# One two-bank PSUM tile for every second pair of units, or two tiles of one bank each

## The chip, the cores and the metric

The kernel runs on one core of a Trainium2 chip. Its time is device microseconds (us) from start to end of one execution; the time before is the median of three runs. The profile and its trace come from one more execution. Engines are written as the profile writes them: PE (TensorE, matmuls), PEld (its weight loads), DVE (VectorE), ACT (ScalarE), POOL (GpSimd) and SP (SyncE, which issues most DMAs). PSUM, the memory that matmuls write, has eight banks of 512 float32 columns on each of 128 partitions.

## The reference

Three layers follow each other; the output is that of the last.

```python
# 1. linear attention with a delta rule: B=4, H=8, S=768, D=48
k_n = k / (norm(k) + 1e-6); state = zeros(B, H, D, D)
for t in range(S):
    y[t] = q[t] @ state
    state += beta[t] * outer(k_n[t], v[t] - state.T @ k_n[t])
# 2. x: 3072 tokens x 384; hidden layer of 2048 with a rational activation
h = x @ w_in
g = (a0 + a1*h + a2*h*h + a3*h*h*h) / (1 + |b0|*|h| + |b1|*h*h + 1e-6)
x = g @ w_out
# 3. 8 experts (384 -> 1024 -> 384, ReLU); each token goes to one expert, at most
#    384 tokens an expert, given out greedily from the highest logit downwards
out[mask_e] = relu(x[mask_e] @ w1[e]) @ w2[e]
```

## The kernel before, in words

The sequence is cut into 12 chunks of 64 steps, so a chunk has 256 tokens (4 batches). The attention of a chunk is a dozen groups of small float32 matmuls into the PSUM tile `tg` (two banks), each read back by ACT or DVE before the next group can use it. It gives the chunk's `xT`. The hidden layer of a chunk is done in 8 **units** of 256 hidden features, 96 units in all. One unit is, in this order:

- `h`, line 906: 18 matmuls of 256 columns (fp16 high and low halves, three products) into the unit's own PSUM tile `P` of one bank;
- the activation, 128x512 at a time, on ACT and DVE by turns. From `P`: L892 `w` (ACT), L889 `q` (ACT), L895 `q` (DVE), L898 and L899 `w` (DVE). Then `P` is used as scratch: L877 and L878 write it (ACT), L881 reads it (DVE), L879 writes it (DVE) and L883 reads it for the last time (DVE). L896 works on `q` alone;
- `gg`, the fp16 high half on ACT (L869) and the low half on DVE or POOL (L870);
- `x2`, line 853: 12 matmuls that add to the chunk's output in `px` (two banks).

A unit takes about four steps of the software pipeline, so four `P` tiles are in use by turns. Units 0 and 1 of each four take the two buffers of a pool, named `ph` in the profile, one bank each. Units 2 and 3 take the halves of `rec`, **one tile of two banks**, cut in two by slicing (`rec0`, `rec1`):

```python
bk[n]=pool.tile([128,1024],F32,name=n)                                    # L1448, n = "tg", "rec"
for i in range(2): bk["%s%d"%(n,i)]=bk[n][:,512*i:512*i+512]
```

While chunk 0 is prepared, `rec` as a whole holds the results of attention groups; its last such use is chunk 0's output `y`, read by ACT and DVE (L1434, L1435) into `xs`. From the first unit with number 2 on, `rec` holds halves only.

The order of the instructions on each engine is set when the kernel is built, by a planner (`Sched`) with a table of durations and priorities; it treats the halves as two banks that have nothing to do with each other. The semaphores are added later by a framework that looks at which instructions write and read which tile. POOL solves small triangular systems for pairs of chunks (L203, L204), with the results going through DRAM (`dA` in, `dW` out). Fill-in matmuls without use (`hot`, L1454) keep PE busy in some of its waits in the first part.

The execution has these parts: up to 67.8 us no unit runs; from 73.8 us (first matmul of a unit into `rec`) to 246 us units of chunks 0 to 2 run beside the preparation of weights; from 246 to 636 us eight chunks, 3 to 10, run in a regular loop; the last chunk's units end by about 690 us; then routing and experts, which use no `rec`.

Of the kernel before, what the change touches and what calls it, by code (L numbers as in the profile page):

```python
# [7 lines left out]
F32 = mybir.dt.float32  # L8
# [6 lines left out]
PSUM = bass.MemoryType.PSUM  # L15
# [495 lines left out]
class Ring:  # L511
# [7 lines left out]
    px=[-381.55,-1154.14,-2703.93,-1331.31,375.89,-100.94,-55.85,-813.57],  # L519
# [206 lines left out]
class Experts:  # L726
# [27 lines left out]
    def split(s,n,q,x,xn,h,l,hn,ln,sc):  # L754

        g=s.g; nc=s.nc; p=PR['sp'][n]+PR['sq'][n]*q
        g.add(('ACT',.43,lambda: nc.scalar.activation(h,x,AF.Copy,scale=sc)),[xn],[hn],p)
        g.add(('DVE',.47,lambda: nc.vector.scalar_tensor_tensor(l,x,sc,h,op0=OP.mult,op1=OP.subtract)),[xn,hn],[ln],p+PR['sl'][n])  # L758
# [84 lines left out]
def units(g,M,T,u0,xT,newP,NP,O):  # L843
# [72 lines left out]
    half=7,  # L916
# [158 lines left out]
def prologue(g,A,M,xT,yev,pack,stg,stx,bk):  # L1075

    nc=A.nc; te,ac,ve,po,sp=nc.tensor,nc.scalar,nc.vector,nc.gpsimd,nc.sync; T={}; LPF=[False]
# [14 lines left out]
    def mm(dur,fn,banks,r,w,pr,act=None):  # L1092

        box=[]
        def f():
            o=A.tg,A.rec; A.tg,A.rec=Banks(),Banks(); A.tg.q,A.rec.q=[bk[b] for b in banks if b[0]=='t'],[bk[b.replace('rt','t')] for b in banks if b[0]=='r']; M.tg=A.tg; A.pend=[]; fn(); A.tg,A.rec=o; M.tg=A.tg; box.extend(A.pend); A.pend=[]
        add(('PE',dur,f),r,w,pr,act=act); return box
    def ev(box,k,eng,dur,r,w,pr): add([('DVE',.6,lambda: box[k](False)),('ACT',.5,lambda: box[k](True))] if eng=='AD' else (eng,dur,lambda: box[k]()),r,w,pr)
# [104 lines left out]
    b=mm(1.7,a12,['rec'],['tn','Ut1'],RE,c0,act=256); ev(b,0,'ACT',.6,RE,['X'],c0)  # L1203
    b=mm(1.7,lambda: A.comb2(0),['rec'],['X',('TT',1),('TT',3)],RE,c0,act=256)
    ev(b,0,'ACT',.55,RE,[('TT',4)],c0); ev(b,1,'AD',.6,RE,[('TT',5)],c0)
    b=mm(2.3,lambda: A.tr(0),['tg'],TD+[('V',0)],TG,cr,act=3072)
# [96 lines left out]
        ev(b,0,'DVE',.081,['tg0'],[('Lt',c)],PP['xo']+8)  # L1303
    id16=A.id16; o,o1=Opt(),Opt(); o.N=DM if ONE else DX; o.K=3; o.stop=False; o.new=o1.new=lambda n,un: M.wk.tile([128,512],F32,name=n,bufs=Opt.R[n]); o.XP,o.HP,o.QP,o.GP,o.SP,o.wi,o.wo=PP['XP'],PP['HP'],PP['QP'],PP['GP'],(0,9),lambda fb,j: [('wi',fb//4,j),('xT',0)],lambda fb: [('wo',fb)] if ONE else [('wo',fb),('wgl',fb)]
    o1.N=DX; o1.K=3; o1.stop=False; o1.XP,o1.HP,o1.QP,o1.GP,o1.SP,o1.wi,o1.wo=PP['XP1'],PP['HP1'],PP['QP1'],PP['GP1'],(0,9),lambda fb,j: [('xT',1)],lambda fb: [('wgl',fb)] if ONE else []
    def newP4(un): return M.ph.tile([128,2,256],F32,name="ph") if un%4<2 else bk['rec%d'%(un%2)].rearrange("p (a b) -> p a b",b=256)
    o.PQ=o1.PQ=PP['PQ']
    U_=[units(g,M,T,0,lambda: xT[0],newP4,4,o),units(g,M,T,8,lambda: xT[1],newP4,4,o1)]; hv=(0,1)
    first=len(g.t)
    add(('DVE',.7,lambda: A.comb0(1)),TD[:4],['tn'],s1_[0])  # L1310
# [11 lines left out]
    for c in range(2):  # L1322
        st=step(c+1)
        for u in range(8):
            un=8*c+u
# [89 lines left out]
def body(ctx,tc,q,k,v,beta,w_in,w_out,a,b,w_gate,w1,w2,out):  # L1415
    nc=tc.nc
    ctx.enter_context(tc.manual_schedule())
    per=ctx.enter_context(tc.tile_pool(name="per",bufs=1))
    drm=ctx.enter_context(tc.tile_pool(name="x2dram",bufs=1,space=DRAM))
    x2d=drm.tile([B*S,DM],F32,name="x2d")  # L1420
    Lt=per.tile([128,E,NT],F32,name="Lt"); nc.gpsimd.memset(Lt,0.0)
    keep=ctx.enter_context(tc.tile_pool(name="keep",bufs=1)); ppx=ctx.enter_context(tc.tile_pool(name="ppx",bufs=2,space=PSUM))
    with ExitStack() as ph1:
        tg=ph1.enter_context(tc.tile_pool(name="ptg",bufs=1,space=PSUM))
        rec=ph1.enter_context(tc.tile_pool(name="prec",bufs=1,space=PSUM))
        pph=ph1.enter_context(tc.tile_pool(name="pph",bufs=2,space=PSUM))
        n=NCK*128*1024; A=Att(ph1,tc,q,(k[0:n].rearrange("(a b) -> a b",b=1024),k[n:].rearrange("(a b) -> a b",b=U*48)),v,beta,tg,rec)
        M=Moe(ph1,tc,w_in,w_out,a,b,w_gate,tg,pph,ppx,keep)
        xw=ph1.enter_context(tc.tile_pool(name="xw",bufs=2))
        xT={}  # L1430
        def yev(c,P,k):
            if c and k==0: xT['s']=xw.tile([128,2,1024],F16,name="xs",bufs=1)
            hi,lo=[xT['s'][:,i] for i in range(2)]; src=P.rearrange("a r p t -> a (r p t)")
            if k==0: nc.scalar.activation(hi,src,AF.Copy,scale=XS)  # L1434
            else: nc.vector.scalar_tensor_tensor(lo,src,XS,hi,op0=OP.mult,op1=OP.subtract)  # L1435
        def pack(c):
            xs=xT['s'].rearrange("p l (s t) -> p l s t",s=4)
            x=xT[c]=xw.tile([128,2,3,256],F16,name="xT")
            for o,n,a,j,i in ((0,48,0,slice(0,3),slice(0,3)),(48,48,64,slice(0,3),slice(0,3)),(96,32,0,0,3),(96,16,32,1,3),(112,16,64,1,3),(96,32,80,2,3)): nc.sync.dma_start(x[o:o+n,:,j],xs[a:a+n,:,i])
        warm=xw.tile([128,256],F16,name="warm",bufs=1); nc.vector.memset(warm,0.0)  # L1440
        M.pools(ph1)
        with ExitStack() as pro:
            ws=pro.enter_context(tc.tile_pool(name="mws",bufs=1,side="right"))
            M.ws=ws; stx=ws.tile([128,FF//2,2],I32,name="wsi")
            stg=[M.wk.tile([128,512],F32,name=n,bufs=b) for n,b in (("sa",2),("sa",2),("q",2),("q",2),("w",3),("w",3),("w",3),("y",2),("y",2))]
            xT['s']=xw.tile([128,2,1024],F16,name="xs",bufs=1); bk={}
            for n,pool in (("tg",tg),("rec",rec)):
                bk[n]=pool.tile([128,1024],F32,name=n)  # L1448
                for i in range(2): bk["%s%d"%(n,i)]=bk[n][:,512*i:512*i+512]
            A.bk=bk  # L1450
            for n,pool,tag in (("P",pph,"ph"),("px",ppx,"px")):
                for i in range(2): bk["%s%d"%(n,i)]=pool.tile([128,512],F32,name=tag)
            def hot(n,t=None):
                for _ in range(n): nc.tensor.matmul((bk['px1'] if t is None else t)[:,0:256],warm[:,0:128],warm,start=True,stop=True)  # L1454
            hot(H00)
            g=Sched(); g.nc=nc; g.tol=PP['tol']; g.free.update(SP=0.6,POOL=3.2,DVE=2.5,ACT=2.0,PE=2.5)
            g.x2d,g.Lt=x2d,Lt; g.mid=lambda: hot(2); T,i1=prologue(g,A,M,xT,yev,pack,stg,stx,bk); i0=next(i for i,t in enumerate(g.t) if t[0][0][0]=='PE'); i1=max(i for i in range(len(g.t)) if g.t[i][0][0][0]=='PE')
            run(g,hot,i0,i1,0,HM,HG,[(('px',1),bk['px1'])]+[(b,bk[b]) for b in ('tg0','tg1')]+[(('P',2+i,0),bk['rec%d'%i]) for i in range(2)])
        rc=ctx.enter_context(tc.tile_pool(name="rc0",bufs=1,side="right"))
        def route():  # L1460
            T['R']=Route(ctx,tc,rc); T['R'].Lt=Lt
        e=g.end; on=g.on; z={x: max([e[i] for i in range(len(e)) if on[i]==x]) for x in ('PE','DVE','ACT','POOL')}; g2=Sched(); g2.nc=nc; g2.x2d,g2.Lt=x2d,Lt; g2.tol=LP['tol']; g2.free.update({x: max(0.0,z[x]-z['PE']+1.0) for x in z})
        T['loop'](g2,route)
        def emit(t,i,f):
            if f: f()
        g2.run(emit); R=T['R']; un=8*(NCK-1)
        G1={un-1: (T['q',un-1],T['w',un-1],T['P',un-1].rearrange("p a b -> p (a b)"))}; G2={un-2: T['w',un-2]}; G3={un-3: T['gg',un-3]}; PX={NCK-2: T['px',NCK-2]}
        g=R.g=Sched(); g.nc=nc
        i0,i1,T=drain(g,M,A,R,(G1,G2,G3,PX[NCK-2]),xT[NCK-1],x2d,Lt); spare=[]
        def hot(n):  # L1470
            if n and not spare: spare.append(M.ph.tile([128,2,256],F32,name="ph"))
            for _ in range(n): nc.tensor.matmul(spare[0][:,0],R.one,warm2,start=True,stop=True)
        warm2=R.hotx
        run(g,hot,i0,i1,EH)
    with ExitStack() as ph2:
        rps=ph2.enter_context(tc.tile_pool(name="rps",bufs=1,space=PSUM))
        eph=ph2.enter_context(tc.tile_pool(name="eph",bufs=1,space=PSUM))
        R.rings(ph2,rps)
        X=Experts(ph2,tc,w1,w2,out,x2d,eph,T['px',NCK-1],M.wof_)
        R.late(ph2)  # L1480
        nc.gpsimd.tensor_scalar(X.ident,R.jp,0.0,None,op0=OP.is_equal); nc.gpsimd.tensor_scalar(X.neg,X.ident,-1.0,None,op0=OP.mult)
        g=tail(R,X,M,T); g.nc=nc; g.free['POOL']=6.0; g.free['ACT']=2.0
        def hot(n):
            for _ in range(n): nc.tensor.matmul(X.ph.t[3][:,:256],R.one,warm2,start=True,stop=True)
        run(g,hot,0,X.first)


body = with_exitstack(body)

_INS = ["q", "k", "v", "beta", "moe_w_in", "moe_w_out", "moe_a", "moe_b", "moe2_w_gate", "moe2_w1", "moe2_w2"]  # L1490
# [58 lines left out]
```

## Time and profile before

| | |
|---|---|
| runs | 970.15 us median (969.09, 970.15, 974.95) |
| profiled execution, its own time | 968.28 us |
| its span, first to last instruction | 966.5 us |
| granted TensorE clock, mean | 0.959 of full |
| PE / DVE / ACT / POOL busy, share of the span | 87% / 80% / 59% / 41% |
| from the loop's start to its end (246 to 636 us) | 390 us, eight chunks, 48.75 us each |

Busy is the time in which an engine had an instruction in work. A row of the waits says for how long an engine stood idle before an instruction, and which instruction of which engine ended the idle time. An idle time counts only if the end of the program hangs on it.

### The profile page before, as it was taken

How to read it: one execution, taken by the hardware profiler on the slowest of the kernel's cores; microseconds unless marked ns; L12 is line 12 of the kernel's file. 1: busy time of each engine (PE TensorE's matmuls, PEld its weight loads, DVE VectorE, ACT ScalarE, POOL GpSimd, SP SyncE). 2: the span in 40 equal slices, each digit the busy share in tenths (PEclk: the TensorE clock that was granted, in tenths of full speed). 3: DMA queues.
4: the chain of work that ended last, by engine and by line, in shares of the span. 5: the costliest groups of instructions: out<-in, count | busy, mean ns of one | idle time of the engine just before them, and what ended most of it. 6: DMA issues, size and time to landing. Idle time of an engine off the chain costs nothing.

```text
span 966.5 us, 29613 instructions
## 1 busy us (share of the span) xinstructions
PE 840.6 (87%) x12504; PEld 589.7 (61%) x12504; DVE 768.8 (80%) x1712; ACT 565.6 (59%) x1027; POOL 392.0 (41%) x591
## 2 busy tenths in 40 slices
PE   8978887879898898889888988888879979999996
PEld 6857655657666566556666666665555545555563
DVE  7898797868788778778877868878678989998930
ACT  3338666767767677668676768767226344533721
POOL 3278527841476376726661111112322214223611
PEclk9979898989999899999998999999899989999999
DMA  8852462305433332433040201000054225443700
GB/s 309 274 156 69 122 149 52 96 24 132 104 90 104 64 92 76 136 36 83 25 119 9 52 2 34 12 6 18 1 173 154 103 81 184 160 164 136 258 25 25
DMA packets 88342, 94.45 MB, mean 98 GB/s; under 512 B 65552, under 2 KB 73360, under 8 KB 85392
## 3 DMA queue, kind: packets, MB, share of 16 engines
q1 hardware_dynamic: 82112, 55.32, 21.9%
q0 software_dynamic: 6096, 37.23, 10.4%
q8 instruction: 98, 1.61, 0.7%
q14 instruction: 36, 0.29, 0.1%
HBM read 70.24 MB, written 17.30 MB: 91 GB/s over the span
## 4 chain that ended last, share of the span: by engine, by line
PE 34%; DVE 27%; ACT 15%; DMA 11%; issue 9%; POOL 2%; SPq 1%; POOLq 0%; ACTq 0%; DVEq 0%
PE rec L906 9%; PE px L853 6%; PE eph L799 4%; PE ph L906 3%; DVE w L881 3%; PE px L812 3%; DMA w1f<-in_moe_w_dram,ix 2%; ACT rec L877 2%; DMA dA<-ka 2%; DVE w L899 2%; DVE q L895 2%; ACT w L892 2%; DVE rec L879 2%; DMA xg<-x2d,perm 2%; DVE w L898 2%
## 5 line engine op out<-in xcount | busy, mean ns | idle before, releaser
L906 PEld LDWEIGHTS <-wi 128*128 128x128 f16 x1728 | 169.6, 101 | 103.1 <-issue 65.8
L853 PE MATMUL px<-wo,gg 128*128 128x392 f16 (+1 forms) x1116 | 206.5, 331 | 5.5 <-DVE wo L1183 2.7
L906 PE MATMUL rec<-xT,wi 128*128 128x256 f16 x864 | 119.9, 286 | 52.6 <-ACT rec L878 8.7
L870 POOL TENSOR_TENSOR gg<-w,gg 128x512 f16<-128x512 f32 x55 | 63.8, 1160 | 221.2 <-ACT gg L869 177.1
L853 PEld LDWEIGHTS <-gg 128*128 128x128 f16 x1116 | 106.5, 98 | 72.1 <-issue 7.9
L906 PE MATMUL ph<-xT,wi 128*128 128x256 f16 x864 | 111.6, 281 | 5.9 <-DMA xT<-xs 3.9
L204 POOL TENSOR_TENSOR pmW<-pmW,pmT 128x31 f32<-128x31 f32 (+15 forms) x155 | 91.0, 587 | 11.1
L203 POOL TENSOR_TENSOR pmT<-pmW,pmA 128x31 f32<-128x31 f32 (+15 forms) x155 | 84.5, 545 | 11.2
L812 PEld LDWEIGHTS <-rr 128*128 128x128 f16 x576 | 52.3, 97 | 33.0 <-issue 2.5
L802 ACT ACTIVATE rr<-eph 128x384 f16<-128x384 f32 x64 | 30.9, 490 | 60.6 <-PE eph L799 56.8
L817 POOL DMA_INDIRECT out_dram<-yo,perm x24 | 28.0, 1166 | 81.9 <-ACT yo L814 79.7
L869 ACT ACTIVATE gg<-w 128x512 f16<-128x512 f32 x88 | 54.8, 623 | 9.3 <-DVE w L883 8.8
L896 ACT ACTIVATE q<-q 128x512 f32<-128x512 f32 x88 | 54.8, 623 | 5.4 <-DVE q L895 4.9
L799 PE MATMUL eph<-xe,w1s 128*128 128x384 f16 x288 | 56.1, 341 | 1.0 <-ACT xe L790 1.0
L812 PE MATMUL px<-w2s,rr 128*128 128x384 f16 x288 | 53.9, 325 | 1.4 <-ACT yo L814 1.4
L812 PE MATMUL px<-wo,rr 128*128 128x384 f16 x288 | 51.2, 325 | 1.7 <-DVE wo L758 1.1
L799 PE MATMUL eph<-xe,wo 128*128 128x384 f16 x288 | 49.8, 325 | 0.0
L889 ACT ACTIVATE q<-ph,cf 128x512 f32<-128x512 f32 x44 | 30.2, 685 | 33.5 <-DVE rec L879 23.1
L804 DVE SCALAR_TENSOR_TENSOR rr<-eph,rr 128x384 f16<-128x384 f32 x57 | 31.2, 552 | 20.0 <-ACT rr L802 18.5
L892 ACT ACTIVATE w<-rec,cf 128x512 f32<-128x512 f32 x44 | 34.2, 777 | 21.9 <-PE rec L906 11.4
L881 DVE SCALAR_TENSOR_TENSOR w<-w,cf,rec 128x512 f32<-128x512 f32 x44 | 32.7, 744 | 17.7 <-PE rec L906 7.6
L895 DVE SCALAR_TENSOR_TENSOR q<-q,cf,rec 128x512 f32<-128x512 f32 x44 | 32.6, 743 | 16.0 <-ACT rec L877 7.8
(379 smaller groups left out, 1860.1 us busy)
## 6 DMA issues: line engine op xcount, KB each, us to landing
kt<-in_k_dram SPq DMA_DIRECT2D x12, 512.0 KB, 4.2
dA<-ka SPq DMA_DIRECT2D x10, 512.0 KB, 3.8
kn<-in_k_dram SPq DMA_DIRECT2D x12, 384.0 KB, 3.9
vn<-in_v_dram SPq DMA_DIRECT2D x12, 384.0 KB, 3.5
qt<-in_q_dram SPq DMA_DIRECT2D x24, 192.0 KB, 3.4
x2d<-xr SPq DMA_DIRECT2D x44, 96.0 KB, 2.2
xT<-xs SPq DMA_DIRECT2D x24, 144.0 KB, 2.7
wsi<-in_moe_w_in_dram SPq DMA_DIRECT2D x3, 1024.0 KB, 6.6
```

Source lines behind the costliest of these rows:

```text
L203: if half==0: eng.tensor_tensor(t,W[:,0:r,j:j+1].to_broadcast([n,r,k]),A[:,j:j+1,j+1:32].to_broadcast([n,r,k]),op=OP.mult)
L204: else: eng.tensor_tensor(W[:,0:r,j+1:32],W[:,0:r,j+1:32],t,op=OP.subtract)
L799: g.add(('PE',.163,lambda P=P,wh=wh,xh=xh,j=j,f=f,part=part: nc.tensor.matmul(P,W1[:,wh,f,j],xe[:,xh,j],start=(part,j)==(0,0),stop=(part,j ...
L812: g.add(('PE',.163,lambda P=P,rh=rh,wh=wh,f=f,part=part,i=i: nc.tensor.matmul(P,r[:,rh,f,128*i:128*i+128],W2[:,wh,f],start=(f,part)==(0,0) ...
L853: te.matmul(T['px',un//8][bp][:,0:O.N],gg()[:,gh,i,128*bp:128*bp+128],M.wo[:,wh,fb,0:O.N],start=fb==0 and n==0,stop=fb==15 and n==2,skip_g ...
L869: ac.activation(T['gg',un][:,0].rearrange("p f t -> p (f t)")[:,a:b],T['w',un][:,a:b],AF.Copy)
L870: def gl(e): return lambda: e.tensor_tensor(T['gg',un][:,1].rearrange("p f t -> p (f t)")[:,a:b],T['w',un][:,a:b],T['gg',un][:,0].rearrang ...
L881: add(('DVE',.07+.6*z,lambda: ve.scalar_tensor_tensor(w(),w(),cf[:,0:1],y(),op0=OP.add,op1=OP.mult)),W+Y,W,un+O.pd('w3',un))
L892: ac.activation(w(),P(),AF.Identity,bias=cf[:,2:3],scale=cf[:,3:4])
L895: add(('DVE',.07+.6*z,lambda: ve.scalar_tensor_tensor(q(),q(),cf[:,4:5],P(),op0=OP.add,op1=OP.mult)),Q+Pn,Q,un+O.pd('mu',un))
L896: add(('ACT',.18+.37*z,lambda: ac.activation(q(),q(),AF.Abs)),Q,Q,un+O.pd('f2',un))
L906: for wh,xh in ((0,0),(0,1),(1,0)): te.matmul(T['P',un][:,i],M.wi[:,wh,part,128*fb:128*fb+128],xT()[:,xh,part],start=n==0,stop=n==8); n+=1
```

## The change

`rec` stays one tile of two banks as long as chunk 0's attention uses it. When the first unit with number 2 of its four asks for a `P` tile, the pool of `rec` is closed and a new pool is opened in the same space, with two tiles of one bank each, `half0` and `half1`; all later units with number 2 and 3 use these. So that the pool can be closed, it is opened after the `ph` pool (its banks become the last two). `hot` gets a bank's name instead of the slice, since the slice behind the name changes.

```diff
-    def newP4(un): return M.ph.tile([128,2,256],F32,name="ph") if un%4<2 else bk['rec%d'%(un%2)].rearrange("p (a b) -> p a b",b=256)
+    def newP4(un):
+        if un%4<2: return M.ph.tile([128,2,256],F32,name="ph")
+        if bk['rec'] is not None: bk['split']()
+        return bk['rec%d'%(un%2)].rearrange("p (a b) -> p a b",b=256)
...
-        rec=ph1.enter_context(tc.tile_pool(name="prec",bufs=1,space=PSUM))
         pph=ph1.enter_context(tc.tile_pool(name="pph",bufs=2,space=PSUM))
+        joint=ph1.enter_context(ExitStack()); rec=joint.enter_context(tc.tile_pool(name="prec",bufs=1,space=PSUM))
...
+            def split():
+
+                joint.close(); p=joint.enter_context(tc.tile_pool(name="psplit",bufs=1,space=PSUM))
+                for i in range(2): bk["rec%d"%i]=p.tile([128,512],F32,name="half%d"%i)
+                bk["rec"]=None
+            bk['split']=split
...
-                for _ in range(n): nc.tensor.matmul((bk['px1'] if t is None else t)[:,0:256],warm[:,0:128],warm,start=True,stop=True)
+                for _ in range(n): nc.tensor.matmul(bk[t or 'px1'][:,0:256],warm[:,0:128],warm,start=True,stop=True)
```

No instruction is added, taken away or moved: the order on every engine is the same, row for row. What differs is which instructions wait for which engine. In the rows below the bracket at the end names the engines for whose semaphore an instruction waits; a number behind a name tells tiles of one name apart.

The first place is on DVE in chunk 5. In the three rows that name `rec_158`, it is the upper half, which holds unit 43; PE is at that time writing unit 46 into the lower half. Before:

```order
L881 SCALAR_TENSOR_TENSOR w_5969<-w_5969,cf_131,rec_158 128x512 [waits Activation_49]
L879 SCALAR_TENSOR_TENSOR rec_158<-q_5982,rec_158 128x512 [waits DVE_49,PE_49]
L898 TENSOR_TENSOR w_6051<-w_6051,ph_5909 128x512 [waits Pool_49]
L883 SCALAR_TENSOR_TENSOR w_5969<-rec_158,w_5969 128x512 [waits DVE_49,PE_49]
L895 SCALAR_TENSOR_TENSOR q_6165<-q_6165,cf_131,ph_6019 128x512 [waits Activation_49]
L277 COPY jn_127<-tg_157 128x2 [waits PE_49]
L899 SCALAR_TENSOR_TENSOR w_6051<-w_6051,cf_131,ph_5909 128x512 [waits DVE_49]
```

The same place with the change:

```order
L881 SCALAR_TENSOR_TENSOR w_5975<-w_5975,cf_131,half1_1207 128x512 [waits Activation_49]
L879 SCALAR_TENSOR_TENSOR half1_1207<-q_5988,half1_1207 128x512
L898 TENSOR_TENSOR w_6057<-w_6057,ph_5915 128x512 [waits Pool_49]
L883 SCALAR_TENSOR_TENSOR w_5975<-half1_1207,w_5975 128x512 [waits DVE_49]
L895 SCALAR_TENSOR_TENSOR q_6171<-q_6171,cf_131,ph_6025 128x512 [waits Activation_49]
L277 COPY jn_127<-tg_157 128x2 [waits PE_49]
L899 SCALAR_TENSOR_TENSOR w_6057<-w_6057,cf_131,ph_5915 128x512 [waits DVE_49]
```

L879 and L883 no longer wait for PE.

The second place is on ACT, at the turn from chunk 7 to chunk 8, where units 62 and 63 are in their activation at the same time, one in each half; L877 and L878 occur once for each. Before:

```order
L869 ACTIVATE gg_134<-w_7660 128x512 [waits DVE_49]
L896 ACTIVATE q_7910<-q_7910 128x512 [waits DVE_49]
L877 ACTIVATE rec_158<-q_7786,cf_131 128x512 [waits DVE_49,Activation_49]
L878 ACTIVATE rec_158<-rec_158 128x512 [waits DVE_49]
L892 ACTIVATE w_7974<-ph_7852,cf_131 128x512 [waits Pool_49]
L877 ACTIVATE rec_158<-q_7910,cf_131 128x512 [waits DVE_49]
L878 ACTIVATE rec_158<-rec_158 128x512 [waits DVE_49]
```

With the change:

```order
L869 ACTIVATE gg_134<-w_7666 128x512 [waits DVE_49]
L896 ACTIVATE q_7916<-q_7916 128x512 [waits DVE_49]
L877 ACTIVATE half0_1206<-q_7792,cf_131 128x512 [waits DVE_49,Activation_49]
L878 ACTIVATE half0_1206<-half0_1206 128x512 [waits Activation_49]
L892 ACTIVATE w_7980<-ph_7858,cf_131 128x512 [waits Pool_49]
L877 ACTIVATE half1_1207<-q_7916,cf_131 128x512 [waits DVE_49]
L878 ACTIVATE half1_1207<-half1_1207 128x512 [waits Activation_49]
```

Each L878 now waits for its own L877 on ACT alone; before, it also waited for a DVE instruction on the other half.

## Rows read from the trace of the kernel before

**Rows 1.** The page, costliest groups: count, busy us, mean ns; idle before, releaser.

```profile
L906 PE MATMUL rec<-xT,wi 128*128 128x256 f16 x864 | 119.9, 286 | 52.6 <-ACT rec L878 8.7
L906 PE MATMUL ph<-xT,wi 128*128 128x256 f16 x864 | 111.6, 281 | 5.9 <-DMA xT<-xs 3.9
```

**Rows 2.** Stretches: length, then PE, PEld, DVE, ACT, POOL busy; PEclk; DMA.

```profile
73.00:246.00 173.00, 146.19 (x2944) 110.28 (x2943) 141.77 (x245) 119.48 (x210) 91.51 (x164) 0.94 0.36 93
204.00:246.00 42.00, 40.24 (x918) 30.29 (x911) 32.62 (x50) 30.92 (x53) 8.87 (x23) 0.95 0.42 107
246.00:636.00 390.00, 342.84 (x6052) 247.80 (x6050) 310.56 (x481) 276.54 (x463) 181.53 (x262) 0.98 0.27 63
438.00:490.00 52.00, 47.09 (x1021) 34.82 (x1019) 44.37 (x67) 38.41 (x63) 33.75 (x50) 1.00 0.27 65
```

**Rows 3.** Groups of PE in the loop, 246 to 636 us.

```profile
L906 PE MATMUL rec<-xT,wi 128*128 128x256 f16 x576 | 80.2, 286 | 40.7 <-ACT rec L877 7.7 <-DVE w L881 7.6 <-ACT rec L878 7.2
L906 PE MATMUL ph<-xT,wi 128*128 128x256 f16 x576 | 70.6, 273 | 2.0 <-DVE w L883 2.0
```

**Rows 4.** Timeline, 380 to 386 us, PE and DVE: start, us, instruction, idle before.

```profile
380.57 0.75 DVE L881 SCALAR_TENSOR_TENSOR w<-w,cf,rec 128x512 f32<-128x512 f32 x1
381.37 0.81 PE L906 MATMUL rec<-xT,wi 128*128 128x256 f16 x6 [0.90 <-DVE w L881]
382.22 0.69 DVE L879 SCALAR_TENSOR_TENSOR rec<-q,rec 128x512 f32<-128x512 f32 x1 [0.91 <-PE rec L906]
...
382.97 1.14 PE L906 MATMUL rec<-xT,wi 128*128 128x256 f16 x9 [0.79 <-DVE rec L879]
...
384.15 0.69 DVE L883 SCALAR_TENSOR_TENSOR w<-rec,w 128x512 f32<-128x512 f32 x1 [0.64 <-PE rec L906]
```

**Rows 5.** Timeline, 497 to 503 us, ACT and DVE.

```profile
497.83 0.69 ACT L877 ACTIVATE rec<-q,cf 128x512 f32<-128x512 f32 x1 [0.69 <-DVE w L898]
...
498.55 0.75 DVE L899 SCALAR_TENSOR_TENSOR w<-w,cf,rec 128x512 f32<-128x512 f32 x1 [0.82 <-ACT rec L877]
...
499.33 0.58 ACT L878 ACTIVATE rec<-rec 128x512 f32<-128x512 f32 x1 [0.82 <-DVE w L899]
...
501.46 0.69 DVE L879 SCALAR_TENSOR_TENSOR rec<-q,rec 128x512 f32<-128x512 f32 x1 [0.76 <-ACT rec L877]
```

**Rows 6.** Tile rec, DVE, loop: idle before its instructions until, us, times.

```profile
  PE rec L906: 27.8, 26
  ACT rec L877: 12.2, 13
  ACT rec L878: 7.5, 13
  ACT w L892: 6.0, 11
  ACT q L889: 5.2, 10
  ACT ph L877: 1.7, 1
  ACT q L896: 1.1, 1
```

**Rows 7.** Tile ph, DVE, loop: the same list, whole.

```profile
  ACT w L892: 4.3, 5
  ACT q L889: 2.4, 1
  ACT ph L878: 2.1, 3
```

**Rows 8.** Groups of PE: rec from 73 to 246 us, then rec and ph from 636.

```profile
L906 PE MATMUL rec<-xT,wi 128*128 128x256 f16 x216 | 29.2, 280 | 5.8 <-ACT rec L878 1.5 <-ACT w L892 1.1 <-DVE w L883 1.0
L906 PE MATMUL rec<-xT,wi 128*128 128x256 f16 x72 | 10.5, 304 | 6.2 <-DVE ut L895 2.7 <-DVE q L879 1.7 <-ACT sbd L892 1.0
L906 PE MATMUL ph<-xT,wi 128*128 128x256 f16 x72 | 8.4, 273 | 0.0
```

**Rows 9.** Tiles rec and ph, DVE, loop: one instruction's ns, min/median/max.

```profile
L881 DVE SCALAR_TENSOR_TENSOR w<-w,cf,rec x32: 733/747/749, 253.6 to 621.4; 128x512 f32<-128x512 f32 x32
L881 DVE SCALAR_TENSOR_TENSOR w<-w,cf,ph x33: 704/742/749, 245.3 to 629.5; 128x512 f32<-128x512 f32 x33
```

**Rows 10.** Timeline of POOL: one pair's solve, from its first product to its output.

```profile
432.70 2.35 POOL L194 TENSOR_TENSOR pmA<-pmA,ss 128x1024 f32<-128x1024 f32 x1
...
500.08 0.59 POOL L207 DMA_DIRECT2D dW<-pmW  x1
```

More of the change, by code (lines that the diff above doesn't have):

```diff
@@ L1457, in body @@
             g.x2d,g.Lt=x2d,Lt; g.mid=lambda: hot(2); T,i1=prologue(g,A,M,xT,yev,pack,stg,stx,bk); i0=next(i for i,t in enumerate(g.t) if t[0][0][0]=='PE'); i1=max(i for i in range(len(g.t)) if g.t[i][0][0][0]=='PE')
-            run(g,hot,i0,i1,0,HM,HG,[(('px',1),bk['px1'])]+[(b,bk[b]) for b in ('tg0','tg1')]+[(('P',2+i,0),bk['rec%d'%i]) for i in range(2)])
+            run(g,hot,i0,i1,0,HM,HG,[(('px',1),'px1')]+[(b,b) for b in ('tg0','tg1')]+[(('P',2+i,0),'rec%d'%i) for i in range(2)])
         rc=ctx.enter_context(tc.tile_pool(name="rc0",bufs=1,side="right"))
```

## The prediction, written before the change was run

> **What bounds the kernel now.** I read first the page's costliest groups, because they hold a comparison that the kernel makes by itself. The units' first matmuls, line 906, go half of the time into the two `ph` buffers and half of the time into the halves of `rec`. The work is the same: 864 matmuls each, of one shape. Yet PE was busy for 111.6 us with the ones and 119.9 with the others, and stood idle for 5.9 us before the ones (3.9 of these for one DMA at the start) and 52.6 before the others [rows 1]. In PE's time `rec` costs 119.9 + 52.6 - 111.6 - 5.9 = 55.0 us more than `ph`. The first thing to see is that pair of rows: same instruction, same count, another tile.
>
> Then I read the stretches. In the regular loop, 390 us for eight chunks, PE is busy 342.84 us (87.9%), DVE 310.56 (79.6%) and ACT 276.54 (70.9%) [rows 2]. No engine is full, PE comes nearest, and it has 47.2 us of idle time. Of that, 40.7 us stand before matmuls into `rec` and 2.0 before those into `ph` [rows 3]. So the wait that ends last in the loop, as far as PE goes, is nearly always one on `rec`.
>
> The timelines show which wait it is. At 380.57 us DVE works on unit 43 in the upper half (L881). PE has unit 46 to write into the lower half, which nobody reads, and starts 0.90 us late, when that DVE instruction has ended. Then DVE's L879 on the upper half waits 0.91 us for PE's six matmuls into the lower one, PE waits 0.79 us for L879, and L883 waits 0.64 us for PE [rows 4]. They take turns on a tile of which each uses another half. At 497.83 us ACT and DVE do the same with units 62 and 63: four instructions, each on the other half than the one before it, each waiting 0.69 to 0.82 us [rows 5]. The framework keeps order by tile, and the tile is both halves. The planner that wrote the order knew nothing of this.
>
> DVE pays as well. In the loop it stood idle for 61.5 us before instructions that name `rec` (the seven numbers added), 27.8 of it until a matmul into `rec` ended; before those that name `ph`, as many in number, it was 8.8 us (the three numbers added), and no matmul is in that list [rows 6, 7].
>
> **The change part by part.**
>
> *Nothing is added.* No engine gets an instruction more or in another place. I followed the semaphores of both programs through, what each instruction must have seen finished directly or through others: with the change it is never more, but for two ScalarE instructions at one place whose buffer of `w` was used by a later POOL instruction. Closing the pool emits nothing on an engine. The first write to a half still waits for L1435, the last reader of chunk 0's output, as before; I cost it at nothing. What the change could lose must come from durations, not from waits.
>
> *The waits between the halves go.* In the loop I put the gain between two ends.
>
> - Upper end: `rec` becomes as good as `ph`. PE then saves 80.2 + 40.7 - 70.6 - 2.0 = 48.3 us [rows 3], and the loop takes 341.7 us. PE would be 97.5% busy (333.2 of 341.7) and DVE 90.9%.
> - Lower end: DVE, which PE must wait for when a `P` tile is to be used again (L883 reads it last), gets no fuller than in the fullest stretch that the trace shows, 44.37 of 52 us, 85.3% [rows 2]. Its 310.56 us then take 364.0, and the loop saves 26.0.
>
> The stretch from 204 to 246 us lies nearer to the upper end: there PE was busy for 40.24 of 42 us, 95.8% [rows 2]. The loop's 333.2 us of PE at that share take 347.8, a saving of 42.2. But DVE had 77.7% to do in that stretch, and would have 89% in the loop. Between 26.0 and 42.2 and 48.3 I take 38.
>
> Before the loop, from 73 to 246 us, `rec` has 216 matmuls with 5.8 us of idle time before them and no longer mean than in the loop [rows 8]. Chunk 1 is held there by the preparation of weights, so part of it will be waited for elsewhere: between 0 and 5.8 I take 3. After the loop, from 636 us, 72 matmuls into `rec` hold PE for 10.5 + 6.2 us and 72 into `ph` for 8.4 [rows 8]; the last chunk is mostly a chain of DVE and ACT, whose turns on the halves go too. Between 0 and 8.3 I take 4. Up to 73 us, and in routing and experts, I expect the same time.
>
> The sum is 38 + 3 + 4 = 45 us, with ends at 26 and 62.4. The profiled execution, 968.28 us by its own clock, would be 923; its time is 1.87 us under the median of the runs, so the median becomes 970.15 - 45 = 925 us.
>
> **The rivals.**
>
> *Half of it is given back.* In-order engines that run closer together find other waits. The place: PE's L906 into a half, now waiting for the L883 of the unit that had this half four units ago. Before `ph` such waits are 2.0 us in the loop [rows 3], with DVE at 79.6%; at 85 to 89% they grow. If DVE stays at 85.3%, 26 us are left in the loop, and perhaps 3 around it: 941 us. A second candidate is POOL's solve of a pair, a chain of its own: from 432.70 to 500.08 it takes 67.4 us [rows 10], and has two chunks, 97.5 us, to do it in. It would have some 88 with the forecast, so I don't count on it.
>
> *DVE is the pace, and PE gives way.* PE's busy time is no fixed load: broken groups cost more, 286 against 273 ns a matmul [rows 3]. If the loop follows DVE's work and its waits that have nothing to do with `rec`, it loses the excess of rows 6 over rows 7, 52.7 us, and with 5.8 and 8.3 around it the kernel takes 903 us. For it speaks that DVE and ACT lose their waits as well; against it that PE would need 333.2 of 337.3 us. The Trainium skill, Perfetto Trace Analysis, "Identifying the Most-Contended Engine", says that matmul busy time is a poor measure of PE's headroom and that weight-load busy time should be taken. By it PE has 247.80 us in the loop [rows 2] and DVE is the most contended engine; with nothing but DVE's work left, the loop would lose up to 79 us. I give this weight only as far as the rival goes, since weight loads here run beside matmuls that are themselves issued back to back.
>
> *The clock falls, and the kernel gets slower.* The granted clock was 0.98 in the loop and 1.00 in a stretch in which PE was busy for 90.6% [rows 2]; its two levels are 2.4 and 1.2 GHz, and the lower one doubles a matmul's time. If PE, no longer paced by `rec`, ran ahead and then stood in fewer but longer waits, the clock could fall. To end 1% above the time before, it would have to eat the 45 us and 9.7 more: about 55 us of the loop's matmul work at the lower level, a sixth of it, a mean clock near 0.86; the time would be 980 us. Against it: the change takes idle time away, and less idle time went with a higher clock from 0.94 before the loop to 1.00 [rows 2]. The Trainium skill, TensorE: Matmul & The Clock Gate, "A second HAM failure mode: psum-queue depth-cycling", tells of a kernel that went round the PSUM banks and idled a little at each turn, so that its clock went up and down. This kernel goes round four `P` tiles before and after, and the trace does not bear that out. That instructions on both halves at once would slow each other is against the rows: DVE's L881 takes 747 ns on `rec` and 742 on `ph`, where nothing held them apart [rows 9].
>
> *It does not do what it says.* If the framework still kept the halves in order, for instance because they lie in a space that was one tile, the time would stay at 970. The rows of the order speak against it, L879 has lost its wait altogether.
>
> **How the numbers follow.** A difference of 1% is about what a measurement of this kernel can tell from no change. I give the forecast (908 to 937, likeliest 925) a chance of 0.65, half given back (937 to 955, at 941) 0.17, DVE as the pace (under 908, at 903) 0.10, no effect 0.05, slower by the clock 0.03. The range is 905 to 947: all of the forecast, most of the case at 941, and the fringe of the one at 903. Faster by over 1% means under 960.4: 0.65 + 0.17 + 0.10 = 0.92; within 1% 0.05; slower 0.03.
>
> **What would show it.** In the trace of the changed kernel, L906 into `half0` and `half1` should have an idle time before it like that of `ph`, under 10 us in the loop, and the same mean; matmuls into a half should be gone from what DVE's and ACT's instructions on the other half wait for. The loop's eight chunks should take about 352 us, 44 each, with PE at 94 to 96% and DVE at 88%, and a clock of 0.98 or more. The part before 73 us and the one after the last unit should keep their lengths. The prediction is wrong if PE's idle time stays near 47 us before other instructions than these, if a part outside the units changes its length by more than 3 us, or if the mean of DVE's instructions grows.

## Result, and the profile after

The changed kernel takes 895.28 us (median of four runs: 888.76, 895.2, 895.35, 899.04), the kernel before 969.92 beside it. The ratio is 0.9213, with a 95% interval of 0.9151 to 0.9276. The gain is 75 us where 45 were forecast, and the time lies 10 us below the range. The profiled execution is the slowest of the four, 899.04 us by its own clock, 69.2 less than the profiled one of before.

Cut at the first matmul of line 906 of a chunk, the two traces give this:

| part | before, us | after, us | saved | forecast (ends) |
|---|---|---|---|---|
| to the loop's start | 245.8 | 237.5 | 8.3 | 3 (0 to 5.8) |
| loop, chunks 3 to 10 | 390.3 | 338.2 | 52.1 | 38 (26.0 to 48.3) |
| last chunk, to its last matmul of line 906 | 33.6 | 27.1 | 6.5 | 4 (0 to 8.3) |
| the rest | 296.8 | 294.5 | 2.3 | 0 |

The first part holds a stretch that got longer: the first unit starts at 69.1 us instead of 67.8. From there to the loop's start 9.6 us are saved.

The page's groups answer to [rows 1]. The two groups of line 906 have changed places:

```profile
L906 PE MATMUL ph<-xT,wi 128*128 128x256 f16 x864 | 114.5, 286 | 11.1 <-DMA xT<-xs 5.7
L906 PE MATMUL half<-xT,wi 128*128 128x256 f16 x864 | 107.6, 275 | 2.9 <-DVE w L883 2.9
```

The loop by itself, columns as in [rows 2]:

```profile
237.52:575.68 338.16, 330.45 (x6053) 245.61 (x6052) 308.32 (x483) 272.75 (x465) 181.76 (x262) 0.99 0.31 73
```

PE is busy for 330.45 of 338.16 us, 97.7%; its idle time fell from 47.2 to 7.7 us. DVE stands at 91.2%, the clock at 0.99. The matmul groups of this stretch, beside [rows 3]:

```profile
L853 PE MATMUL px<-wo,gg 128*128 128x392 f16 x805 | 146.3, 329 | 0.0
L906 PE MATMUL ph<-xT,wi 128*128 128x256 f16 x576 | 72.5, 278 | 5.5 <-DVE w L883 5.5
L906 PE MATMUL half<-xT,wi 128*128 128x256 f16 x576 | 70.3, 273 | 2.2 <-DVE w L883 2.2
...
L258 PE MATMUL tg<-sbd,kt 48*64 48x48 f32 x512 | 9.2, 220 | 0.0
L267 PE MATMUL tg<-vn,tt 64*64 64x48 f32 x512 | 9.2, 220 | 0.0
```

Before, the same answer (245.79 to 636.06 us) had idle time also in front of two groups that have nothing to do with `rec`:

```profile
L853 PE MATMUL px<-wo,gg 128*128 128x392 f16 x805 | 147.8, 332 | 0.0
...
L258 PE MATMUL tg<-sbd,kt 48*64 48x48 f32 x512 | 9.2, 220 | 2.6 <-ACT tt L249 2.4 <-DVE tt L250 0.2
L267 PE MATMUL tg<-vn,tt 64*64 64x48 f32 x512 | 9.2, 220 | 1.9 <-DVE vn L259 1.9
```

The list of what DVE waited for before instructions that name a half, which answers to [rows 6], is down from 61.5 us to 4.5, and no matmul is in it:

```profile
  ACT q L889: 1.8, 4
  ACT half L878: 1.5, 4
  ACT w L892: 1.2, 5
```

The place of [rows 4] looks so now (the rows of DVE, then the one of PE; L879 is the one that waited 0.91 us for PE, and the fifteen matmuls are those that were broken into six and nine):

```profile
358.93 0.74 DVE L881 SCALAR_TENSOR_TENSOR w<-w,cf,half 128x512 f32<-128x512 f32 x1
359.59 0.69 DVE L879 SCALAR_TENSOR_TENSOR half<-q,half 128x512 f32<-128x512 f32 x1
360.19 0.68 DVE L898 TENSOR_TENSOR w<-w,ph 128x512 f32<-128x512 f32 x1
360.79 0.68 DVE L883 SCALAR_TENSOR_TENSOR w<-half,w 128x512 f32<-128x512 f32 x1
...
359.34 1.81 PE L906 MATMUL half<-xT,wi 128*128 128x256 f16 x15
```

None of the four waits of [rows 4] is left. PE writes the lower half while DVE's L881 and L879 work on the upper one. It is so elsewhere too: counted from the two traces between 100 and 570 us, no two engines were ever at work on `rec` at one time before; after, PE and DVE were on the two halves at once for 15 us, PE and ACT for 16, DVE and ACT for 29.

### The profile page after: what moved, and what is told of

Same layout as the page of the kernel before. It is cut to its first block, busy times and chain, and to the rows that moved or that the text cites. A ratio compares the mean times of both kernels' runs of the same rounds, so it can differ in the third digit from the quotient of the medians.

```text
span 897.2 us, 29591 instructions
## 1 busy us (share of the span) xinstructions
PE 827.4 (92%) x12504; PEld 589.0 (66%) x12504; DVE 762.1 (85%) x1712; ACT 559.1 (62%) x1027; POOL 390.6 (44%) x591
## 5 line engine op out<-in xcount | busy, mean ns | idle before, releaser
L853 PE MATMUL px<-wo,gg 128*128 128x392 f16 (+1 forms) x1116 | 204.5, 329 | 4.6 <-DVE wo L1183 2.2
L906 PEld LDWEIGHTS <-wi 128*128 128x128 f16 x1728 | 167.3, 100 | 47.7 <-DVE w L883 6.0
L853 PEld LDWEIGHTS <-gg 128*128 128x128 f16 x1116 | 106.1, 98 | 69.8 <-issue 6.2
L906 PE MATMUL ph<-xT,wi 128*128 128x256 f16 x864 | 114.5, 286 | 11.1 <-DMA xT<-xs 5.7
L906 PE MATMUL half<-xT,wi 128*128 128x256 f16 x864 | 107.6, 275 | 2.9 <-DVE w L883 2.9
L812 PEld LDWEIGHTS <-rr 128*128 128x128 f16 x576 | 52.7, 98 | 33.3 <-issue 3.6
L746 POOL DMA_INDIRECT w1f<-in_moe_w_dram,ix x8 | 7.8, 976 | 83.8 <-DVE ic L667 49.8
L1463 PEld LDWEIGHTS <-warm 128*128 128x128 f16 x335 | 33.7, 106 | 14.9 <-issue 4.8
L895 DVE SCALAR_TENSOR_TENSOR q<-q,cf,ph 128x512 f32<-128x512 f32 x44 | 32.5, 738 | 12.8 <-ACT w L892 8.7
```

The lines of the kernel that those rows point to most:

```text
L812: g.add(('PE',.163,lambda P=P,rh=rh,wh=wh,f=f,part=part,i=i: nc.tensor.matmul(P,r[:,rh,f,128*i:128*i+128],W2[:,wh,f],start=(f,part)==(0,0) ...
L853: te.matmul(T['px',un//8][bp][:,0:O.N],gg()[:,gh,i,128*bp:128*bp+128],M.wo[:,wh,fb,0:O.N],start=fb==0 and n==0,stop=fb==15 and n==2,skip_g ...
L906: for wh,xh in ((0,0),(0,1),(1,0)): te.matmul(T['P',un][:,i],M.wi[:,wh,part,128*fb:128*fb+128],xT()[:,xh,part],start=n==0,stop=n==8); n+=1
L1463: for _ in range(n): nc.tensor.matmul(bk[t or 'px1'][:,0:256],warm[:,0:128],warm,start=True,stop=True)
```

## The experiments

**Is it the waits?** The first four kernels are the changed one with links put back between the halves. A link makes an instruction on one half wait for the latest instruction of another engine on the other half (for a read: the latest that wrote there). `KEEP` says which engine waits for which. Instructions and their order stay as they were; line 906 becomes 922 in these four kernels and 926 in those of runs 6 to 8. Costs over the split kernel are differences of medians; by the ratios they come out the same within 4 us.

```diff
+    def __call__(s,un,e,write,ins):
+        if un%4<2: return ins
+        x=un%2
+        for (y,f),last in list((s.a if write else s.w).items()):
+            if y!=x and f!=e and (e,f) in Links.KEEP:
+                Links.tc.add_manual_dep(ins.ins,last.ins.name,mybir.DependencyInfo(mybir.DependencyClass.Sync,mybir.DependencyReason.DATA),reason="other half")
+        s.a[x,e]=ins
+        if write: s.w[x,e]=ins
+        return ins
...
-            ac.activation(q(),P(),AF.Abs,scale=cf[:,5:6])
+            LK(un,'ACT',0,ac.activation(q(),P(),AF.Abs,scale=cf[:,5:6]))
...
```

*1. All pairs of engines.*

> The split tiles, with every wait between the halves put back by explicit links (PE on DVE and ACT, DVE and ACT on PE, DVE and ACT on each other). Theory, the waits between the halves are the whole difference: 970 us, 962 to 978. Rival, the banks' new places or the later opening of the pool give a part (the gain was 75 us where 45 were forecast): then that part stays, and the time is 935 to 955.

954.57 us, ratio 0.9837 (0.9783 to 0.989). It is short of the kernel before by 15 us, at the edge of the rival's range. Either the banks have a share or the links lack something; runs 5 and 6 decide between the two.

*2. Only PE waits.* `KEEP=[('PE','DVE'),('PE','ACT')]`

> The split tiles, with only those links put back in which PE, about to write one half, waits for DVE and ACT on the other. Theory A, the count of the prediction (PE's own idle time before rec is the cost, about 46 us of idle time in the trace of before): nearly all comes back, 940 us or more. Theory B, the turns are a game of three engines, and PE waits long only because DVE and ACT were themselves held up by PE: a part comes back, 15 to 35 us, 910 to 930 us.

899.27 us, 0.926 (0.9199 to 0.932): 4 us over the split kernel, which its interval doesn't tell from nothing. Both theories fall. In the loop PE stood idle before a half for 7.0 us, not 40.7:

```profile
L922 PE MATMUL half<-xT,wi 128*128 128x256 f16 x576 | 74.1, 278 | 7.0 <-ACT half L893 4.7 <-ACT q L912 0.9 <-ACT half L894 0.5
```

*3. Only DVE and ACT wait for PE.* `KEEP=[('DVE','PE'),('ACT','PE')]`

> The split tiles, with only those links put back in which DVE and ACT wait for PE's matmuls into the other half. Theory A: PE itself waits for no half, so the time stays within 10 us of the split kernel, 890 to 905 us. Theory B: DVE stood idle for 27.8 us in the loop of before until matmuls into the other half ended, and ACT some 17 us; this delays the last read of a tile and so PE: 15 to 45 us come back, 910 to 940 us.

895.01 us, 0.9209 (0.9152 to 0.9266): nothing comes back. A is right here, but not for its reason, which run 2 has refuted. DVE's wait for PE on the other half is in the trace, only short:

```profile
  PE half L922: 5.8, 9
```

*4. Only DVE and ACT wait for each other.* `KEEP=[('DVE','ACT'),('ACT','DVE')]`

> The split tiles, with only those links put back by which DVE and ACT wait for each other across the halves. Theory A: 890 to 905 us. Theory B: these are the rarest on the chain; 5 to 20 us come back, 900 to 915 us.

910.29 us, 0.9395 (0.9336 to 0.9455): 15 us come back, as B had it. The three add up to 19 us, and all together (run 1) cost 59. Run 3 cost nothing, so a link as such has no price that shows. So the waits work on each other, and a third theory is needed: **one side that waits loses little, because it comes late once and then stays behind; two sides that wait for each other, in a ring, lose a turn every time they meet.** Run 7 tests what this costs; that coming late once is how the first half comes about is argued, not shown.

*5. The banks' places.* The split is left out, the order of the pools kept:

```diff
         if un%4<2: return M.ph.tile([128,2,256],F32,name="ph")
-        if bk['rec'] is not None: bk['split']()
         return bk['rec%d'%(un%2)].rearrange("p (a b) -> p a b",b=256)
```

> The pools opened in the order of the changed kernel, but the tile never split, so that rec lies in the last two banks and every wait is that of before. If the banks' places had a part in the gain, 935 to 960 us; if they had none, 965 to 975 us.

969.9 us, 1.0017 (0.9983 to 1.0052). The banks' places have no part in the gain that the interval shows.

*6. The full set of links.* With the banks excluded, the missing 15 us had to be waits. The joint tile orders more than run 1 did: a read by DVE on one half waits for a read by ACT on the other, and DVE and ACT wait for their own last instruction on the other half (a read only if that one wrote). Links of both kinds are added:

```diff
-        for (y,f),last in list((s.a if write else s.w).items()):
-            if y!=x and f!=e and (e,f) in Links.KEEP:
+        for (y,f),last in list(s.a.items()):
+            if y!=x and ((f!=e and (e,f) in Links.KEEP and (write or True or s.w.get((y,f)) is last)) or (f==e and True and f!='PE' and (write or s.w.get((y,f)) is last))):
...
```

> The split tiles, with all links of the first run and two kinds more that the joint tile also had: reads of the two halves by DVE and ACT are kept in order too, and an engine waits for its own last access to the other half. If the waits are the whole difference, 965 to 975 us. If the 15 us that the first run was short of the kernel before come from the banks, it stays at 950 to 960 us.

972.42 us, 1.0046 (1.0015 to 1.0077), 77 us over the split kernel: the waits are the whole difference. The interval lies just above 1, and the loop took 394.0 us against 390.3, so the links hold back slightly more than the tile did; where is open. That the joint tile kept reads in order is in the traces, between 100 and 570 us: a read by DVE on one half ran beside a read by ACT on the other 23 times in the changed kernel, 20 times in run 1, and never in the kernel before or in run 6. The loop has its old rows back, with `half` where `rec` stood:

```profile
L926 PE MATMUL half<-xT,wi 128*128 128x256 f16 x576 | 81.0, 288 | 41.5 <-ACT half L898 7.4 <-ACT half L897 6.5 <-ACT w L912 4.9
```

*7. Both directions between PE and the others.* `KEEP` of runs 2 and 3 together.

> The links of the second and third run together: PE waits for DVE and ACT on the other half, and they for PE, but DVE and ACT not for each other. Apart these cost 4 and 0 us. If costs add up, 893 to 904 us. If the turns cost only as a ring, in which both sides wait for each other, 915 to 945 us.

931.4 us, 0.9597 (0.9552 to 0.9641): 36 us, against 4 and 0 apart. This is the ring, as expected. PE's idle time before a half and DVE's until PE has written the other half are both 26.1 us, some four times what each was alone, and DVE waits 27 times instead of 9:

```profile
L926 PE MATMUL half<-xT,wi 128*128 128x256 f16 x576 | 75.0, 274 | 26.1 <-ACT half L898 5.1 <-ACT w L912 4.9 <-DVE half L899 4.8
```

```profile
  PE half L926: 26.1, 27
```

*8. DVE and ACT with the full set between them.*

> DVE and ACT wait for each other across the halves, with the order of reads and an engine's waits for itself as in the full set; PE free of links in both directions. The smaller set cost 15 us; this one 920 to 935 us if the order of reads is what the first run lacked, 908 to 915 if not.

922.23 us, 0.9521 (0.9473 to 0.9569): 27 us instead of 15. So the order of reads and the waits of an engine for itself cost 12 us between DVE and ACT alone; with all links on (run 6 against run 1) they cost 18, which covers the missing 15. Which of the two kinds it is was not taken apart. 36 and 27 make 63 of run 6's 77 us; the other 14 come only when both rings are closed.

**Which engine sets the pace?** The lower end of the forecast feared DVE. Four kernels leave out work in the loop, once on PE (its busy time there falls by 33 us, where 47 were expected) and once on DVE (by 36 to 37 us, where 43 were expected), after and before. The rest keeps its order.

```diff
-                for wh,xh in ((0,0),(0,1),(1,0)): te.matmul(T['P',un][:,i],M.wi[:,wh,part,128*fb:128*fb+128],xT()[:,xh,part],start=n==0,stop=n==8); n+=1
+                for wh,xh in ((0,0),(0,1)): te.matmul(T['P',un][:,i],M.wi[:,wh,part,128*fb:128*fb+128],xT()[:,xh,part],start=n==0,stop=n==5); n+=1
```

```diff
-        add(('DVE',.07+.535*z,lambda: ve.tensor_tensor(w(),w(),P(),op=OP.mult)),W+Pn,W,un+O.pd('w1',un))
+        add(('DVE',.07+.535*z,lambda: None),W+Pn,W,un+O.pd('w1',un))
```

*9.* 

> The changed kernel with one of the three products of line 906 left out (12 matmuls a unit instead of 18, so h is less exact): about 47 us less PE work in the loop, 74 in all. If PE is what the loop follows now (97.7% busy there, DVE 91%), the loop falls to DVE's pace, 15 to 25 us less, and 5 to 10 us go outside it: 862 to 876 us. If DVE and ACT already hold the pace, as the prediction's lower end had it, 885 to 897 us.

874.0 us, 0.9021 (0.8979 to 0.9064): 21 us less than the split kernel. The loop is 14 us shorter and now at DVE's pace, 305.65 of 324.19 us, 94.3%, while PE waits 10.9 us before the halves (6.4 of them in one wait, at the end of a chain that begins with ACT's wait for a DMA):

```profile
237.37:561.56 324.19, 297.01 (x5669) 208.38 (x5668) 305.65 (x483) 271.31 (x465) 181.79 (x262) 0.98 0.33 76
```

```profile
L906 PE MATMUL half<-xT,wi 128*128 128x256 f16 x384 | 50.5, 277 | 10.9 <-DVE w L883 10.7
```

*10.* 

> The changed kernel with line 898 left out (one of DVE's five reads of P, so the activation is another function): about 43 us less DVE work in the loop. If PE is the pace, at most its 7.7 us of idle time can go there and some in the parts around it: 880 to 895 us. If DVE is the pace, 850 to 865 us.

890.72 us, 0.92 (0.9167 to 0.9233): 5 us less, no difference that the intervals tell. PE is 99% busy in its loop (328.61 of 331.91 us), DVE 82%:

```profile
236.74:568.65 331.91, 328.61 (x6054) 244.72 (x6052) 272.75 (x419) 272.32 (x466) 181.91 (x262) 1.00 0.32 74
```

*11.* 

> The kernel before with the same product left out. PE was its fullest engine too, 88% in the loop. If its idle time was simply added to its work, all of the 47 us go and some outside: 905 to 925 us. If the turns between the halves set the pace, less than half comes out: 940 to 960 us.

951.27 us, 0.9824 (0.979 to 0.9858): 18 us. PE's busy time in the loop fell from 343 to 310 us, the loop by only 12 (378.55 us), and the idle time before `rec` grew from 40.7 to 48.7. The clock in this loop was 0.95, not 0.98, so PE's work fell by more than its busy time shows:

```profile
242.99:621.54 378.55, 309.96 (x5669) 212.49 (x5668) 309.92 (x480) 275.28 (x464) 181.12 (x262) 0.95 0.28 65
```

```profile
L906 PE MATMUL rec<-xT,wi 128*128 128x256 f16 x384 | 58.4, 289 | 48.7 <-ACT rec L877 11.4 <-DVE w L881 8.4 <-ACT rec L878 8.2
```

*12.* 

> The kernel before with line 898 left out, 43 us less DVE work in a loop in which DVE was 80% busy. If the turns set the pace, DVE's work is part of them although it is not the fullest engine: 925 to 955 us, more than the change gains from the same cut in the changed kernel. If only PE's work and its idle time count, 960 to 970 us.

947.17 us, 0.9774 (0.9751 to 0.9798): 22 us, against 5 from the same cut after the change; the loop is 10 us shorter:

```profile
240.89:621.39 380.50, 343.38 (x6055) 248.49 (x6053) 273.76 (x416) 276.63 (x463) 181.49 (x262) 0.97 0.27 64
```

L898 is one of DVE's five reads of `P`, so this cut takes turns away too, not only work. In the kernel before, 33 us less busy time on PE and 37 less on DVE shortened the loop by 12 and 10 us, so neither engine's work alone was the pace; with runs 6 and 7, the turns between them were. In the changed kernel it is PE, with DVE 10 to 14 us behind it in the loop (the lower figure against the loop of run 3, 334.0 us).

## Why the prediction was right, and where it was wrong

- **What bounds the kernel: right.** The waits between the halves cost 75 us and nothing else does (runs 5 and 6). Nothing was added, and no part of the table got longer. That the groups on `rec` and `ph` show the price of the tile held in the loop: `half` has 2.2 us of idle time and a mean of 273 ns, as forecast.
- **The loop: the step that failed.** It is the sentence "Between 26.0 and 42.2 and 48.3 I take 38"; the loop saved 52.1. Both figures that pulled it down were busy shares from stretches of the kernel before: DVE no fuller than 85.3%, PE at 95.8% [rows 2]. The first was misread: the loop before has a stretch of the same length with DVE at 46.65 of 52 us, 89.7%. By it DVE's 310.56 us take 346.2, and the lower end is 43.8, not 26.0. Those stretches also had the turns in them, so the shares said how full an engine got with the turns, not what it can reach without. Afterwards DVE was at 91.2% and PE at 97.7%, and with PE's work cut DVE went to 94.3%. The stretch of the kernel before:

```profile
254.00:306.00 52.00, 46.79 (x1130) 34.77 (x1127) 46.65 (x71) 36.42 (x60) 38.75 (x61) 1.00 0.37 100
```

- **Its upper end was none.** It counted only what PE lost before `rec`. By groups: the halves give 40.7 - 2.2 in idle time and 80.2 - 70.3 in matmul time, 48.4. L258 and L267 give 4.5 more, since the ACT and DVE instructions that they wait for come earlier, and L853 1.5. `ph` takes back 3.5 and 1.9. That makes 49.0; the groups' busy times overlap, and some 3 us of PE's busy time are not to be placed in one.
- **The rows 6 count of DVE** (52.7 us excess) came out nearest to the 52.1, and this was the rival "DVE is the pace", at 903. Its size held, its mechanism did not: DVE's work is not the pace (run 10). PE did give way, by 12 us of busy time in the loop: matmuls that are not broken up take 273 ns, not 286. That the sizes agree so closely is luck: run 3's loop, without the long wait described below, is 56 us shorter than before. The Trainium skill, Perfetto Trace Analysis, "Identifying the Most-Contended Engine", would have PE judged by its share of peak arithmetic and by its weight loads, not by matmul busy time. The weight loads were 245.61 of 338.16 us, 73%, which makes DVE the most contended. Runs 9 and 10 say PE, and here the 97.7% of matmul time told the truth.
- **Before and after the loop: undersized, by 5 and 3 us.** Before the loop I took idle time alone; the mean fell there too, so that 216 matmuls into a half hold PE for 27.4 + 0.7 us, against 29.2 + 5.8 [rows 8]. After the loop 6.5 us is inside the ends. The rest moved by 2.3 us. The group before the loop, after the change:

```profile
L906 PE MATMUL half<-xT,wi 128*128 128x256 f16 x216 | 27.4, 273 | 0.7 <-DVE w L883 0.7
```

- **Half given back: did not happen.** The place named for it, L906 waiting for the L883 of four units ago, is 2.2 us in one wait. The 5.5 us before `ph` are the wait described under the median.
- **The clock: right**, 0.99 in the loop. One argument for it does not hold: less idle time did not go with a higher clock in the stretch from 204 to 246 us, 95.8% busy at 0.95 [rows 2], nor does it after the change, where PE is never idle in the 40 us before the loop and the clock is 0.93:

```profile
197.60:237.52 39.92, 39.92 (x917) 30.15 (x909) 32.55 (x50) 30.01 (x52) 10.21 (x28) 0.93 0.43 110
```

- **The median** lies 3.8 us under the profiled run. That run has a long wait early in the loop. ACT's L96 stands until `pmA` has come back from DRAM; DVE's L102 reads what L96 writes and stands with it, and PE then waits for DVE. (The row of L102 names the load of `kt`, which landed at about that time, but L102 does not read `kt`.) In the trace of run 3 the first two of the waits below are 2.27 and 2.28 us, and in the kernel before 2.14 and 1.97. Run 3's loop took 334.0 us, 56 less than before the change, so some 4 us of the profiled loop are this one wait and nothing of the change. Why it was longer that once stays open.

```profile
245.49 0.35 ACT L96 ACTIVATE ss<-pmA,tiny 128x32 f32<-128x32 f32 x1 [6.71 <-DMA pmA<-dA]
245.87 0.21 DVE L102 TENSOR_TENSOR ss<-pmA,ss 128x32 f32<-128x32 f32 x1 [6.49 <-DMA kt<-in_k_dram]
246.80 4.00 PE L906 MATMUL ph<-xT,wi 128*128 128x256 f16 x18 [5.47 <-DVE w L883]
```

`tg` is also one tile of two banks and is used by halves while the weights are prepared. Whether splitting it pays was not tried: its groups read columns that only the first clearing has written, so the tile can't be given out anew in between.

## What to carry to other kernels

Where several engines work by turns on parts of one tile, look for instructions that wait for an engine busy on another part, and give each part a tile of its own. What such waits cost can't be read off one engine's idle rows, nor bounded by the busy shares of a stretch that has them: a wait in one direction cost 0 to 4 us here, both directions together 36. To know the pace, cut an engine's work and see whether the time follows; in the kernel before, 33 us less busy time on the fullest engine shortened the loop by 12.

## What the runs showed of the hardware

Work in one bank did not slow work in the bank beside it. In the changed kernel's loop PE or ACT was at work on the other half for more than half the time of nine of DVE's L881; these took 742 ns in the mean, and the eighteen beside which nobody was on the other half took 741. ACT's L878 took 585 and 586 ns (17 and 10 of them). Before, when L881 had the two banks of `rec` to itself, its median was 747 ns [rows 9]; the line in the loop now:

```profile
L881 DVE SCALAR_TENSOR_TENSOR w<-w,cf,half 128x512 f32<-128x512 f32 x33 | 24.5, 741 | 1.7 <-ACT half L878 1.5
```

That the framework keeps even reads by two engines in order for a whole tile was unexpected. Its price is part of the 12 us between runs 4 and 8; what part is not shown. The Trainium skill, PSUM — Partial Sum Buffer, "PSUM bank collisions raise a hardware error", says that two engines must not be in the same bank and quadrant at once, reads included; by that the order is needed inside a bank, but not between the two banks of one tile. No run here lets two engines into one bank, so the first half of this is not shown. The second is in line with the changed kernel, in which two engines were in the two banks at once for tens of us, with no L881 or L878 slowed.
